# Moving narrowing calls between the first and the eighth expert, and the norm's squares to other buffers

## The chip, the cores and the metric

The kernel runs on one core of a Trainium2 chip. The metric is the device time of one execution in microseconds (us); lower is better. Engines are named as in the profile: PE multiplies matrices (PEld loads its weights), DVE, ACT and POOL work on vectors, SP issues transfers; ACT and POOL issue some too.

## The reference

Three layers follow one another. The second and third are what this change touches:

```python
# x: 3072 tokens x 384, from a gated linear attention in fp32
def _moe_ref(x, w_gate, w1, w2):          # 8 experts, 384 tokens each, chosen greedily by x @ w_gate
    ...
    for e in range(E):
        mask = assigned == e
        h = np.maximum(x[mask] @ w1[e], 0.0)      # 384 -> 1024
        out[mask] = h @ w2[e]                     # 1024 -> 384
    ...
def _moe2_ref(x, w_gate, w_val, w_out, rms_g):
    rms = np.sqrt(np.mean(x * x, axis=-1, keepdims=True) + 1e-06)
    xn = x / rms * rms_g
    g = xn @ w_gate                               # 384 -> 1536
    silu = g * (1.0 / (1.0 + np.exp(-g)))
    return (silu * (xn @ w_val) @ w_out).astype(np.float32)
```

The three weights of the last layer arrive as 64-bit floats and are made into 32-bit floats on the chip.

## The kernel before

**Products.** Each fp32 operand is split into a high part and the remainder; a product is three matmuls (`mm3`). The split of a weight piece of 128x1536 (768 KB), `piece_split`, is a cast on ACT (L880) and a subtraction (L883) on DVE, for two pieces of the last layer on POOL.

**Experts.** `expert(e)` runs eight slots j = 0 to 7, each on 128 of the 1024 hidden columns. PE computes h[j] (9 matmuls), ACT makes hh (L1161), DVE makes the remainder hl (L1162), and two slots later PE uses both in `second(e, j-2)` (9 matmuls). After h[j] is handled, `side(e, j)` adds the work for what comes next: gathering and turning the next expert's rows (`xpose`), loading and splitting weight pieces, and the narrowing. Each engine runs its instructions in the order in which this code is written.

**Narrowing.** The last layer's weights fall into 36 items, and one call of `narrow_step` does three things, each for another item:

```python
if len(done) > 1 or (done and not ready):
    nc.scalar.dma_start(*done.pop(0))          # write a finished item to DRAM (192 KB), issued by ACT
if len(ready) > 1 or (ready and not todo):
    done.append(narrow2(*ready.pop(0)))        # make a 32-bit item from a loaded one
if todo:
    ready.append(narrow(*todo.pop(0)))         # load a raw item (384 KB), issued by SP into nraw
```

`narrow2` is one multiplication on ACT into the buffer nr (L1080), three DVE instructions into nb and ne (L1081, L1082, L1084) and two POOL instructions on nr (L1085, L1086). An item is loaded in call n, made in call n+2 and written in call n+4; forty calls finish all. nraw and nr have three buffers each and nb two, given out in turn, so the multiplication of an item waits until the item that last used its nr buffer has landed in DRAM (ACT nr L1080 <- DMA w_o<-nr in the views).

**Eighth expert.** There `side` loads and splits the first pieces of the last layer (`w2_load`, `piece_split(W2[j-1])`), and prepares the norm of the first 256 tokens: `squares` in slot 0 (ACT: L983, two L986, and the cast L990; DVE: two additions L987 and a remainder L991), `total` in slot 2 (two PE matmuls L995, L996, and a square root with its table load, L997), then reciprocals, scaling, and in slot 6 a cast on ACT (L1019) and a remainder on POOL (L1020) for each of three parts. The squares are held in nraw buffers. After the eighth expert PE begins the last layer.

Of the kernel before, what the change touches and what calls it, by code (L numbers as in the profile page):

```python
# [7 lines left out]
F32 = mybir.dt.float32  # L8
F32R = mybir.dt.float32r
BF = mybir.dt.bfloat16  # L10
I32 = mybir.dt.int32
# [793 lines left out]
def tile_kernel(ctx, tc, q, k, v, f_logit, w_gate, w1, w2, w2_gate, w2_val, w2_out, rms_g, fT, kT, qT, vL, out):  # L805
# [70 lines left out]
    def piece_split(p, cp=None):  # L876
        pool, raw, shape, eng = p
        hi, lo = (pool.tile([128, 1536], F32R, name="w").rearrange("p (a b) -> p a b", a=shape[0]) for _ in range(2))
        if cp is None:
            nc.scalar.copy(hi, raw)  # L880
        else:
            cp.tensor_scalar(hi, raw, 1.0, 0.0, op0=OP.mult, op1=OP.add)
        eng.tensor_tensor(out=lo, in0=raw, in1=hi.bitcast(F32), op=OP.subtract)  # L883
        p[:] = [(hi, lo)]
# [17 lines left out]
    def gather(e):  # L902
        if e not in XG:
            XG[e] = [xp.tile([128, DM], F32, name="xrow") for _ in range(KD)]
        for c, t in enumerate(XG[e]):
            nc.gpsimd.indirect_dma_start(out=t, out_offset=None, in_=x_dram[:, :],
                                         in_offset=bass.IndirectOffsetOnAxis(
                                             ap=idx[:, 3 * e + c:3 * e + c + 1], axis=0))
# [3 lines left out]
    def w_load(e, i):  # L912
        W1[e, i] = piece(wpool, rawp, *w_src(e, i), nc.vector, e == 1 and i < 2)
# [10 lines left out]
    with ExitStack() as st:  # L924
        with tc.tile_pool(name="rw", bufs=8) as rw, tc.tile_pool(name="rwp", bufs=4, space=PSUM) as rwp:
# [8 lines left out]
            def side(s):  # L934
                if 0 < s < 5:
                    pool, raw, shape, _ = W1[0, s - 1]
                    hi, lo = (pool.tile([128, 1536], F32R, name="w").rearrange("p (a b) -> p a b", a=shape[0])
                              for _ in range(2))
                    nc.scalar.copy(hi, raw)
                    parts[s - 1] = hi, lo, raw  # L940
# [29 lines left out]
    TC = 256  # L970
# [45 lines left out]
    def prep(c, d, X, eng):  # L1016
        s = xn[:, d, c * TC:(c + 1) * TC]
        hi, lo = (t[:, d, 0:TC] for t in X)
        nc.scalar.copy(hi, s)  # L1019
        eng.tensor_tensor(out=lo, in0=s, in1=hi.bitcast(F32), op=OP.subtract)  # L1020

    W2 = {}
    with ExitStack() as c1:
        P = lambda name, bufs, **kw: c1.enter_context(tc.tile_pool(name=name, bufs=bufs, **kw))
        hp = P("m1h", 3, side="right")
        tp = P("m1t", 1, side="right")
        psT = P("m1psT", 2, space=PSUM)
# [4 lines left out]
        def w2_load(i):  # L1032
            if i < 7:
                W2[i] = piece(wpool, rawp, *w2_src(i), nc.gpsimd if i in (1, 3) else nc.vector)
# [3 lines left out]
        def xpose(e, d):  # L1038
            if d == 0:
                XT[e] = xt_tiles()  # L1040
            o = psT.tile([128, CAP], F32, name="xT")
            for c in range(3):
                nc.tensor.transpose(o[:, c * 128:(c + 1) * 128], XG[e][c][:, d * 128:(d + 1) * 128], ident)
            split(e, d, o)
# [15 lines left out]
        def nraw():  # L1060
            return tp.tile([128, 384, 2], I32, name="nraw", bufs=3)
# [30 lines left out]
        def narrow_step():  # L1092
            if len(done) > 1 or (done and not ready):
                nc.scalar.dma_start(*done.pop(0))
            if len(ready) > 1 or (ready and not todo):
                done.append(narrow2(*ready.pop(0)))
            if todo:
                ready.append(narrow(*todo.pop(0)))
# [4 lines left out]
            X0.extend(xt_tiles())  # L1103
            return [t[:, 0, 0:TC] for t in X0]

        n0 = Norm(0, tp, psT, "xT", lambda n: nraw().rearrange("p c two -> p (c two)").bitcast(F32)[:, :TC], first_parts)
        tail0 = n0.steps()[2:]
        NORM0 = {(E - 1, 0): [n0.squares], (E - 1, 2): [n0.total], (E - 1, 3): tail0[0:2], (E - 1, 4): tail0[2:3]}
        del tail0[:3]
# [1 line left out]
        def side(e, j):  # L1111
            if e + 1 < E:
                if j == 0:
                    gather(e + 1)
                    w_load(e + 1, 1)
                if j in ((1, 2, 3, 4, 5) if e == 0 else (1, 3, 5)):
                    narrow_step()
                if 0 < j < 5:
                    piece_split(W1[e + 1, j - 1])
                if j in (1, 2):  # L1120
                    w_load(e + 1, j + 1)
                if j > 4:
                    xpose(e + 1, j - 5)
                if j == 7:
                    if e + 2 < E:
                        w_load(e + 2, 0)
                    else:
                        w2_load(0)
                if j > 5:
                    narrow_step()  # L1130
            else:
                if j < 6:
                    w2_load(j + 1)
                if j in (0, 1, 3):
                    narrow_step()
                if j:
                    piece_split(W2[j - 1])
                if j == 5:
                    for f in tail0:
                        f()  # L1140
                if j == 6:
                    for d in range(KD):
                        prep(0, d, X0, nc.gpsimd)
            for f in NORM0.get((e, j), ()):
                f()
# [190 lines left out]
```

## Time and profile before

| what | value |
|---|---|
| median of three runs | 809.45 us (806.89 to 809.86) |
| the profiled execution | 806.72 us, of which its instructions span 805.0 us |
| PE busy | 784.6 us, 97% of the span |
| DVE, ACT, POOL busy | 474.7, 391.0 and 277.4 us |
| granted TensorE clock | 0.993 on average |

A busy share is an average over stages. Times in the rows further below are counted from the start of the span. The first expert runs from about 141 to 165 us, the eighth from about 324 to 351 us, and the last layer fills the rest.

### The profile page before, as it was taken

The numbers are of one execution on the slowest core, as the hardware profiler recorded it, in microseconds if no ns is written. First come the engines' busy times: TensorE is split into PE (matmuls) and PEld (weight loads), VectorE is DVE, ScalarE is ACT, GpSimd is POOL, SyncE is SP. The second block draws the span as 40 slices with busy tenths as digits, with TensorE's granted clock in tenths as the row PEclk, the third lists the DMA queues.
The fourth block names the chain that finished last, engine by engine and source line by source line (L and its number), as shares of the span: only waits on it lengthen the run. The fifth ranks groups of instructions, "written<-read, shape, count | busy, mean of one in ns | idle before, by whom it ended". The sixth has DMA issues, their size and how long they took to land.

```text
span 805.0 us, 17025 instructions
## 1 busy us (share of the span) xinstructions
PE 784.6 (97%) x6813; PEld 767.3 (95%) x6813; DVE 474.7 (59%) x855; ACT 391.0 (49%) x853; POOL 277.4 (34%) x332
## 2 busy tenths in 40 slices
PE   8999987999999999999999999999999999999996
PEld 7888876999999999999999999999999999999996
DVE  8999885988886768665434343444443443434331
ACT  5888571565456455764434343434434243434221
POOL 7889603377577667430111111110201011111110
PEclk9999997999999999999999999999999999999999
DMA  9999453697667866521000000000000000000000
GB/s 280 219 243 244 167 202 130 240 315 269 238 232 273 296 234 236 208 77 40 20 1 22 1 20 1 21 2 20 20 2 21 2 20 1 21 1 21 1 21 20
DMA packets 44278, 88.60 MB, mean 110 GB/s; under 512 B 5888, under 2 KB 23552, under 8 KB 44192
## 3 DMA queue, kind: packets, MB, share of 16 engines
q1 hardware_dynamic: 35088, 70.90, 27.8%
q0 software_dynamic: 3104, 9.44, 3.2%
q10 hardware_dynamic: 6000, 7.09, 2.5%
q8 instruction: 55, 0.90, 0.5%
q14 instruction: 31, 0.25, 0.1%
HBM read 70.91 MB, written 16.52 MB: 109 GB/s over the span
## 4 chain that ended last, share of the span: by engine, by line
PE 71%; issue 7%; DVE 2%; DMA 2%; POOL 1%; ACT 1%; POOLq 0%; DVEq 0%; ACTq 0%
PE o L686 5%; PE g L685 5%; PE g L686 5%; PE v L686 5%; PE v L687 5%; PE v L685 5%; PE g L687 5%; PE o L685 5%; PE o L687 5%; PE h L686 4%; PE h L687 4%; PE h L685 4%; PE x L686 3%; PE x L687 3%; PE x L685 3%
## 5 line engine op out<-in xcount | busy, mean ns | idle before, releaser
L1261 DVE TENSOR_TENSOR hf<-sg,v 128x256 f32<-128x256 f32 x144 | 59.9, 416 | 179.6 <-PE v L687 132.1
L1264 ACT CAST hh<-hf 128x256 fp32r<-128x256 f32 x144 | 58.6, 407 | 139.3 <-DVE hf L1261 139.3
L1020 POOL TENSOR_TENSOR xlo<-xn,xhi 128x256 fp32r<-128x256 f32 x36 | 29.6, 823 | 275.1 <-ACT xhi L1019 275.1
L686 PE MATMUL g<-xlo,w 128*128 128x256 f32 x432 | 119.3, 276 | 0.0
L685 PE MATMUL v<-xhi,w 128*128 128x256 f32 x432 | 119.2, 276 | 0.0
L686 PE MATMUL v<-xlo,w 128*128 128x256 f32 x432 | 119.2, 276 | 0.0
L687 PE MATMUL g<-xhi,w 128*128 128x256 f32 x432 | 119.2, 276 | 0.0
L687 PE MATMUL v<-xhi,w 128*128 128x256 f32 x432 | 119.2, 276 | 0.0
L685 PE MATMUL g<-xhi,w 128*128 128x256 f32 x432 | 119.2, 276 | 0.0
L1259 ACT ACTIVATE sg<-g 128x256 f32<-128x256 f32 x144 | 55.3, 384 | 98.8 <-PE g L687 98.5
L1265 DVE TENSOR_TENSOR hl<-hf,hh 128x256 fp32r<-128x256 f32 x144 | 61.3, 425 | 68.0 <-ACT hh L1264 63.3
L686 PE MATMUL o<-w,hh 128*128 128x384 f32 x288 | 97.0, 337 | 0.0
L685 PE MATMUL o<-w,hh 128*128 128x384 f32 x288 | 96.6, 335 | 0.0
L687 PE MATMUL o<-w,hl 128*128 128x384 f32 x288 | 96.2, 334 | 0.0
L685 PEld LDWEIGHTS g<-xhi,w 128*128 128x128 f32 x432 | 81.1, 188 | 0.0
L687 PEld LDWEIGHTS g<-xhi,w 128*128 128x128 f32 x432 | 81.1, 188 | 0.0
L685 PEld LDWEIGHTS v<-xhi,w 128*128 128x128 f32 x432 | 81.1, 188 | 0.0
L686 PEld LDWEIGHTS v<-xlo,w 128*128 128x128 f32 x432 | 81.1, 188 | 0.0
L687 PEld LDWEIGHTS v<-xhi,w 128*128 128x128 f32 x432 | 81.1, 188 | 0.0
L686 PEld LDWEIGHTS g<-xlo,w 128*128 128x128 f32 x432 | 81.0, 187 | 0.1
L883 DVE TENSOR_TENSOR w<-wraw,w 128x1536 fp32r<-128x1536 f32 x35 | 68.4, 1954 | 5.3 <-ACT w L880 4.9
L1085 POOL TENSOR_TENSOR nr<-nr,ne 128x384 f32<-128x384 f32 x36 | 52.1, 1446 | 56.3 <-DVE ne L1084 16.2
(247 smaller groups left out, 1869.0 us busy)
## 6 DMA issues: line engine op xcount, KB each, us to landing
wraw<-in_moe_w_dram SPq DMA_DIRECT2D x32, 768.0 KB
v<-in_v_rows_dram SPq DMA_DIRECT2D x16, 288.0 KB
x_dram<-xrows SPq DMA_DIRECT2D x24, 192.0 KB
nraw<-in_moe_w_gate_dram SPq DMA_DIRECT2D x12, 384.0 KB
nraw<-in_moe_w_val_dram SPq DMA_DIRECT2D x12, 384.0 KB
nraw<-in_moe_w_out_dram SPq DMA_DIRECT2D x12, 384.0 KB
raw_f<-in_f_logit_turned_dram SPq DMA_DIRECT2D x26, 144.0 KB
raw_k<-in_k_turned_dram SPq DMA_DIRECT2D x26, 144.0 KB
```

Source lines behind the costliest of these rows:

```text
L685: nc.tensor.matmul(out, lhs[0], rhs[0], start=first, stop=False)
L686: nc.tensor.matmul(out, lhs[0], rhs[1], start=False, stop=False)
L687: nc.tensor.matmul(out, lhs[1], rhs[0], start=False, stop=last)
L883: eng.tensor_tensor(out=lo, in0=raw, in1=hi.bitcast(F32), op=OP.subtract)
L1020: eng.tensor_tensor(out=lo, in0=s, in1=hi.bitcast(F32), op=OP.subtract)
L1085: nc.gpsimd.tensor_tensor(out=r, in0=r, in1=e2.bitcast(F32), op=OP.mult)
L1259: nc.scalar.activation(sg, pg, AF.Silu)
L1261: nc.vector.tensor_tensor(out=h, in0=sg, in1=pv, op=OP.mult)
L1264: nc.scalar.copy(hh, h)
L1265: nc.vector.tensor_tensor(out=hl, in0=h, in1=hh.bitcast(F32), op=OP.subtract)
```

## The change

The number of calls stays forty. Slot 5 of expert 0 (in the code e == 0, j == 5) loses its call. In expert 7 the calls were in slots 0, 1 and 3; they are now in slots 1, 2, 4 and 6. Every call after slot 4 of expert 0 therefore handles the item that the call before it had handled. The squares take buffers from nr (the sum) and nb (the two further squares) and none from nraw.

```diff
@@ -1103,7 +1103,12 @@
             X0.extend(xt_tiles())
             return [t[:, 0, 0:TC] for t in X0]
 
-        n0 = Norm(0, tp, psT, "xT", lambda n: nraw().rearrange("p c two -> p (c two)").bitcast(F32)[:, :TC], first_parts)
+        def first_tmp(n):
+            t = tp.tile([128, 384], F32, name="nr", bufs=3) if n == "ss" else \
+                tp.tile([128, 384], I32, name="nb", bufs=2).bitcast(F32)
+            return t[:, 0:TC]
+
+        n0 = Norm(0, tp, psT, "xT", first_tmp, first_parts)
         tail0 = n0.steps()[2:]
@@ -1113,7 +1118,7 @@
-                if j in ((1, 2, 3, 4, 5) if e == 0 else (1, 3, 5)):
+                if j in ((1, 2, 3, 4) if e == 0 else (1, 3, 5)):
                     narrow_step()
@@ -1131,7 +1136,7 @@
             else:
                 if j < 6:
                     w2_load(j + 1)
-                if j in (0, 1, 3):
+                if j in (1, 2, 4, 6):
                     narrow_step()
```

On DVE in expert 0, before, from hl of slot 5 to hl of slot 7 (hl is L1162, the narrowing L1081 to L1084, the turned rows' remainder L1049):

```order
L1162 SCALAR_TENSOR_TENSOR hl_3343<-h_3332,hh_3342 128x384
L1081 TENSOR_SCALAR nb_3356<-nraw_3288 128x384
L1082 SCALAR_TENSOR_TENSOR nb_3356<-nraw_3288,nb_3356 128x384
L1084 TENSOR_SCALAR ne_3357<-nb_3356 128x384
L1049 TENSOR_TENSOR xlo_3368<-xT_3369,xhi_3367 128x384
L1162 SCALAR_TENSOR_TENSOR hl_3386<-h_3375,hh_3385 128x384
L1049 TENSOR_TENSOR xlo_3368<-xT_3398,xhi_3367 128x384
L1081 TENSOR_SCALAR nb_3405<-nraw_3326 128x384
L1082 SCALAR_TENSOR_TENSOR nb_3405<-nraw_3326,nb_3405 128x384
L1084 TENSOR_SCALAR ne_3406<-nb_3405 128x384
L1162 SCALAR_TENSOR_TENSOR hl_3427<-h_3416,hh_3426 128x384
```

And the same place now (lines below the first edit carry numbers higher by five):

```order
L1167 SCALAR_TENSOR_TENSOR hl_3343<-h_3332,hh_3342 128x384
L1049 TENSOR_TENSOR xlo_3356<-xT_3357,xhi_3355 128x384
L1167 SCALAR_TENSOR_TENSOR hl_3374<-h_3363,hh_3373 128x384
L1049 TENSOR_TENSOR xlo_3356<-xT_3386,xhi_3355 128x384
L1081 TENSOR_SCALAR nb_3393<-nraw_3288 128x384
L1082 SCALAR_TENSOR_TENSOR nb_3393<-nraw_3288,nb_3393 128x384
L1084 TENSOR_SCALAR ne_3394<-nb_3393 128x384
L1167 SCALAR_TENSOR_TENSOR hl_3415<-h_3404,hh_3414 128x384
```

Of the two sets of three narrowing instructions between hl of slot 5 and hl of slot 7, the one behind slot 5 is gone.

On ACT in expert 7, before, from the end of slot 0 (its write and its multiplication L1080, then the squares) through hh of slots 1 and 2 to the second weight split:

```order
L1094 DMA w32_o_64<-nr_5207 128x384
L1080 ACTIVATE nr_5300<-nraw_5214 128x384
L983 ACTIVATE nraw_5307<-xn_3105 128x256
L986 ACTIVATE nraw_5309<-xn_3105 128x256
L986 ACTIVATE nraw_5312<-xn_3105 128x256
L990 CAST xhi_5315<-nraw_5307 128x256
L1161 ACTIVATE hh_5329<-h_5319 128x384
L1094 DMA w32_o_64<-nr_5250 128x384
L880 CAST w_5336<-wraw_5245 128x1536
L1161 ACTIVATE hh_5350<-h_5340 128x384
L880 CAST w_5365<-wraw_5295 128x1536
```

And now, at the same place:

```order
L983 ACTIVATE nr_5287<-xn_3105 128x256
L986 ACTIVATE nb_5289<-xn_3105 128x256
L986 ACTIVATE nb_5292<-xn_3105 128x256
L990 CAST xhi_5295<-nr_5287 128x256
L1166 ACTIVATE hh_5309<-h_5299 128x384
L1094 DMA w32_o_64<-nr_5195 128x384
L1080 ACTIVATE nr_5318<-nraw_5202 128x384
L880 CAST w_5325<-wraw_5233 128x1536
L1166 ACTIVATE hh_5339<-h_5329 128x384
L1094 DMA w32_o_64<-nr_5238 128x384
L1080 ACTIVATE nr_5357<-nraw_5245 128x384
L880 CAST w_5364<-wraw_5285 128x1536
```

The multiplication ahead of the squares is gone, and one now stands ahead of each of the two weight splits. With three nr buffers given out in turn (..., nr_5195, nr_5238, nr_5287 for the squares, nr_5318, nr_5357), nr_5318 is the memory of nr_5195 and nr_5357 that of nr_5238, which the write just ahead of each multiplication reads.

## Rows read from the trace of the kernel before

**Rows 1.** Waits of PE, whole run: us in total, times, longest.

```profile
PE xT L995 <- ACT xhi L990: 1.3, 1, 1.3
PE x L686 <- DVE hl L1162: 1.1, 1, 1.1
```

**Rows 2.** Timeline of DVE, expert 0: start, duration, what, idle before.

```profile
157.66 0.55 DVE L1162 SCALAR_TENSOR_TENSOR hl<-h,hh 128x384 fp32r<-128x384 f32 x1
158.12 0.71 DVE L1081 TENSOR_SCALAR nb<-nraw 128x384 int32<-128x384 int32 x1
158.87 1.25 DVE L1082 SCALAR_TENSOR_TENSOR nb<-nraw,nb 128x384 int32<-128x384 int32 x1
160.22 0.36 DVE L1084 TENSOR_SCALAR ne<-nb 128x384 int32<-128x384 int32 x1
...
164.04 0.55 DVE L1162 SCALAR_TENSOR_TENSOR hl<-h,hh 128x384 fp32r<-128x384 f32 x1
```

**Rows 3.** Timeline of PE, turn of expert 7's slots 2 and 3, and its last hl.

```profile
329.59 0.34 PE L686 MATMUL x<-hl,w 128*128 128x384 f32 x1
329.77 0.34 PE L687 MATMUL x<-hh,w 128*128 128x384 f32 x1
331.43 0.39 PE L995 MATMUL xT<-xhi,onesr 128*128 128x256 f32 x1 [1.32 <-ACT xhi L990]
...
332.11 0.34 PE L685 MATMUL h<-xhi,w 128*128 128x384 f32 x1
...
349.45 0.34 PE L686 MATMUL x<-hl,w 128*128 128x384 f32 x1
```

**Rows 4.** Timeline of ACT, expert 6's slot 7 to expert 7's slot 3.

```profile
320.61 0.33 ACTq L1094 DMA_DIRECT2D w_o<-nr  x1
...
327.57 0.55 ACT L1080 ACTIVATE nr<-nraw 128x384 f32<-128x384 uint32 x1 [1.14 <-DMA w_o<-nr]
328.02 0.40 ACT L983 ACTIVATE nraw<-xn 128x256 f32<-128x256 f32 x1
...
330.97 0.40 ACT L990 CAST xhi<-nraw 128x256 fp32r<-128x256 f32 x1 [1.93 <-DVE nraw L987]
330.98 0.33 ACTq L1094 DMA_DIRECT2D w_o<-nr  x1
...
331.66 1.47 ACT L880 CAST w<-wraw 128x1536 fp32r<-128x1536 f32 x1
...
333.41 1.48 ACT L880 CAST w<-wraw 128x1536 fp32r<-128x1536 f32 x1
...
336.94 1.48 ACT L880 CAST w<-wraw 128x1536 fp32r<-128x1536 f32 x1
```

**Rows 5.** Timeline of DVE, expert 7.

```profile
328.76 2.17 DVE L987 TENSOR_TENSOR nraw<-nraw 128x256 f32<-128x256 f32 x2 [0.40 <-ACT nraw L986]
...
338.44 1.76 DVE L883 TENSOR_TENSOR w<-wraw,w 128x1536 fp32r<-128x1536 f32 x1 [0.80 <-ACT w L880]
...
342.68 2.71 DVE L883 TENSOR_TENSOR w<-wraw,w 128x1536 fp32r<-128x1536 f32 x1
...
348.72 0.55 DVE L1162 SCALAR_TENSOR_TENSOR hl<-h,hh 128x384 fp32r<-128x384 f32 x1
```

**Rows 6.** The tile ss: the same additions of squares in the last layer (min/median/max ns).

```profile
L987 DVE TENSOR_TENSOR ss<-ss,hf x22: 424/426/428, 355.5 to 726.1; 128x256 f32<-128x256 f32 x22
```

**Rows 7.** Windows in expert 7: busy time per engine, PEclk, DMA share, GB/s.

```profile
332.00:332.25 0.25, 0.25 (x2) 0.25 (x3) 0.25 (x1) 0.25 (x1) 0.00 (x0) 1.00 1.00 362
332.25:332.50 0.25, 0.25 (x4) 0.25 (x3) 0.10 (x1) 0.25 (x1) 0.00 (x0) 1.00 0.61 205
332.50:332.75 0.25, 0.25 (x3) 0.25 (x2) 0.00 (x0) 0.25 (x1) 0.00 (x0) 1.00 0.00 0
```

**Rows 8.** Timeline of SP's queue, expert 6's slots 6 and 7.

```profile
315.89 1.33 SPq L873 DMA_DIRECT2D wraw<-w_g  x3
```

**Rows 9.** Timeline of POOL, expert 7.

```profile
334.96 3.51 POOL L883 TENSOR_TENSOR w<-wraw,w 128x1536 fp32r<-128x1536 f32 x1 [4.31 <-ACT w L880]
```

## The prediction

> **What bounds the kernel now.** I read the page first: PE is at work for nearly the whole span. So I went to the list of waits, for PE. Of its sixteen entries, two lie in the experts and none in the last layer [rows 1]: 1.1 us for hl and 1.3 us for the operand of the norm's total. The timelines place them. The first is in expert 0: hl of slot 7 starts on DVE at 164.04 and ends at 164.59, when PE has been waiting for it [rows 2]. DVE ran without a pause from hl of slot 5 to there, and the narrowing of slot 5 took it from 158.12 to 160.58. So in this slot DVE is the bound. The second is in expert 7 [rows 3]: the matmul of `second` at 329.77 is followed by the total at 331.43 and by h[3] at 332.11. Matmuls follow each other here every 0.18 us (329.59 to 329.77), so without a wait the total's two and h[3] would have begun by 330.3, three steps after 329.77: this place costs PE 1.8 to 1.9 us, and I carry 1.9.
>
> Why the total is late is read from ACT [rows 4]. The multiplication at 327.57 waited for a write issued at 320.61, and the squares, begun at 328.02, come behind it. From the squares' start to the cast at 330.97 there are 2.95 us, and 2.17 of them are two DVE additions [rows 5].
>
> What comes next in expert 7 matters as much. ACT then works without a pause from 330.97 to the third weight split at 336.94, and DVE, which waits for that split at 338.44, has no pause from there to hl of slot 7 at 348.72 [rows 5]. That hl ends at 349.27 and PE uses it at 349.45 [rows 3]: PE and the chain ACT, DVE end expert 7 within 0.2 us of each other. Whatever PE gains at the total is worth nothing unless this chain comes earlier too, and whatever delays the third split ends on PE.
>
> **The change part by part.** *Slot 5 of expert 0.* Ahead of hl of slot 7, DVE loses three instructions. They took 2.46 us by their place on the timeline; the same three, by the shortest of their durations there for the last and half or less for the first two, would be 1.3 us, when POOL does not work beside them. Either is enough for the 1.1 us of wait. I count −1.1 us. The bounds are 0, if something else arrives last, and −1.3, with the matmul's own step of 0.18 us on top. Between expert 0 and expert 7 the calls do the same work on other items, and PE waits nowhere there [rows 1], so I cost that at nothing; without this cover a late hl would be paid at the 1.1 us of expert 0.
>
> *Squares.* Their multiplication and POOL's two additions of narrowing no longer lie in slot 0. The DVE additions, 1.04 us each today beside POOL, took 0.43 us each in the last layer, where no narrowing runs [rows 6]. So the way from the squares to the cast shrinks by 1.3 us. When do the squares begin? Their sum now takes the nr buffer that the write of expert 6's slot 7 reads, so they wait for a landing, as the multiplication did. The write issued at that place today landed at 327.5, 6.9 us after its issue [rows 4]: it stood behind the three big loads issued from 315.89 [rows 8] and a fourth. Now a raw load of 384 KB is queued by SP in front of all but the first of these; at the 362 GB/s of [rows 7] it is worth 1.1 us. So the squares begin between 327.5 and 328.6, and I take 328.0, as today.
>
> *Two multiplications behind writes.* In slots 1 and 2 of expert 7 the multiplication waits for the write that ACT issued just before. Let L be the time from issue to landing. Behind the waiting instruction stand the weight split, hh of the next slot, the table load and root, and hh of slot 3. The row for L is the write issued at 330.98 [rows 4] into empty queues: its bytes move until 332.5 [rows 7]. So L is above 1.5 us. The upper bound is the 6.9 us of a write behind big loads. At 330 the big loads are over, so I take a value near the lower one, 2.0 us. It is an estimate: 1.5 us plus some time for the landing to be signalled.
>
> The Trainium skill, in DMA: Bandwidth & Descriptors, section Anatomy of one DMA, gives about 2.0 us of fixed cost plus the bytes at 436 GB/s, most of the fixed part being the receipt of the write; that fit is for transfers that POOL issues. For 192 KB it makes an estimate of L = 2.45 us, where the row shows only the 1.5 us until the last byte; with it the sum below would come out 0.7 us higher.
>
> The first write leaves when the cast at 330.97 starts, since ACT issues a transfer while earlier instructions still run (the write at 330.98). The split that began at 331.66, 0.69 us after the cast, now begins after L and a multiplication of 0.45 us (327.57 to 328.02): L − 0.24, or 1.76 us later. The second write leaves when the first has landed; until its landing ACT has a multiplication (0.45) and a split with an hh (1.75, from 331.66 to 333.41) to do, 2.2 us, so for L below 2.2 only the second multiplication counts, 0.45 us. Together ACT is 2.2 us later. For L = 1.5 it is 1.7.
>
> *POOL beside DVE.* The additions of two items now run on POOL in slots 1 to 3, ahead of the weight remainder that begins at 334.96 [rows 9] and takes 3.51 us. The second of them can't begin before its multiplication and DVE's three instructions (1.3 us or more), and each addition takes about 1 us, as the DVE additions beside them did [rows 5]: from a second multiplication that ends near 335 that makes about 338 to 339 for the remainder, an estimate. So it moves beside the DVE split that begins at 338.44. That split took 1.76 us with POOL idle; the one at 342.68, beside POOL, took 2.71 [rows 5]. I add 0.95 us, bounds 0 and 2.85 for three such splits.
>
> The third split in expert 7, and with it the DVE chain, comes 0 (start of the squares) − 1.3 + 2.2 = 0.9 us later, plus 0.95 for the contention, less the 0.18 us between hl and its use: PE ends expert 7 1.7 us later than today. The 1.9 us at the total are mostly freed, but PE then waits for hl of slots 2 to 7 instead. Writes in slots 4 and 6 wait for items finished long before. They end before the load that reads them in the last layer, so I cost them at nothing; uncovered, the load would be late by one L, 2.0 us.
>
> **Sum.** −1.1 + 1.7 = +0.6 us. On the profiled execution's 806.72 us it gives 807.3; the median of the runs shown is 2.7 us above that execution, and against it the forecast is 810.0 us. A change within 0.5%, 4 us here, is about what a measurement of this kernel cannot tell from none.
>
> **Rivals.** *Both stalls vanish (chance 0.26).* If POOL does not disturb DVE and the squares start early (the write of slot 7 put ahead of the last big load, at about 326 us), the chain comes 2 us earlier and covers the two waits: −1.1 − 1.9 = −3.0, 806.4 us. For it: the raw load splits the big loads, so the write may be issued before the last of them. Against it: SP needs about 0.45 us for each issue [rows 8], which puts the last of them just before the write.
>
> *POOL against DVE (0.09).* With three splits lengthened instead of one the sum is 2 × 0.95 higher: +2.5 us, 812.0. The Trainium skill's GPSIMD Engine Reference, section Key points, says that POOL shares its SBUF interfaces with DVE instructions that read two SBUF inputs, as these splits do; the 1.76 and 2.71 us of [rows 5] agree. By that rule every split beside a POOL instruction pays, and it would give this rival's time. Against it: POOL's two remainders lie beside DVE work today as well.
>
> *Writes behind loads (0.05).* This one ends slower. If big loads are still in the queues at 330 us, L is 6.9 us. The first wait then costs 6.66, the second 0.45 + 6.9 − 2.2 = 5.15, the chain 0.9 − 2.2 + 11.8 = 10.5 us, and the total is −1.1 + 10.5 + 0.95 − 0.18 = +10.2: 819.7 us. It decides from about L = 3.8 us on, where 2L − 2.0 for the two waits brings the sum to +4 us. Against it: the queues are empty at 332.5 [rows 7] and the next big load needs a buffer that the delayed split frees.
>
> *Nothing gained in expert 0 (0.05).* If another instruction, say a turned row's remainder, is last there, the −1.1 is missing: 811.1 us.
>
> **How the numbers follow.** The forecast has 0.55, the rivals 0.26, 0.09, 0.05 and 0.05. All but the writes behind loads stay within 4 us. The forecast's own range is the spread of its terms, L from 1.5 to 2.45 and the squares' start by 0.5 us either way, about 808 to 812. To hold 8 in 10 I reach to the first rival's 806.4 below and past the second's 812.0 above, by the 0.8 us that a late POOL costs: 806.2 to 812.8. Faster by over 0.5% needs more than both stalls: 0.05, for what the terms leave out. Slower by over 0.5%: 0.05 for the late writes and 0.03 for three terms at their upper bounds together. Same: 0.87.
>
> **What would show it.** In expert 0 PE's wait for hl of slot 7 is gone and the experts 0 to 6 end about 1.1 us earlier. The two additions of squares take 0.43 us each, and PE's wait at the total falls below 0.9 us. ACT shows two new waits for w_o<-nr in slots 1 and 2 of expert 7, of 1 to 2 us each, the third split comes later relative to the squares' cast than today's 5.97 us, by about 2.2, and PE waits for hl two or three times in slots 2 to 7. The prediction is wrong if the third split follows the cast by less than 7 us (L is smaller, and the first rival holds) or by more than 10 us, or if the stretch from 165 us to the eighth expert changes its length.

## The result, and the profile after

The changed kernel took 813.17 us (median of 6 runs, 812.86 to 813.77), the kernel before 808.63 us beside it (6 runs, 806.31 to 809.86): ratio 1.0053, 95% interval 1.0035 to 1.0071. It is 4.5 us slower; 0.6 us were forecast, and the range ended at 812.8.

The profiled execution spans 812.1 us, 7.1 more than before's. Cut at PE's first h of expert 0, its last `second` matmul of experts 0 and 6, and its first g of the last layer, the spans show where (PE makes the first two h of expert 0 in smaller pieces, so this cut lies ahead of the 141 us given for the first expert above):

| stage | before, us | after, us |
|---|---|---|
| up to expert 0 | 136.60 | 138.34 |
| expert 0 | 29.36 | 28.04 |
| experts 1 to 6 | 157.44 | 158.52 |
| expert 7 | 27.42 | 32.88 |
| last layer | 454.18 | 454.29 |

The first stage holds the same code in all kernels here, and lay anywhere between 136.6 and 139.3 us in the eighteen profiles. Experts 1 to 6 took 156.8 to 159.0 us in all but two. So these two rows tell nothing; expert 0 (−1.3) and expert 7 (+5.5) do, and add up to 4.1.

The waits of PE, answering to [rows 1]:

```profile
PE x L686 <- DVE hl L1167: 3.8, 2, 3.3
...
PE xT L995 <- ACT xhi L990: 0.3, 1, 0.3
```

Expert 0's wait for hl is gone, the wait at the total fell from 1.3 to 0.3 us, and one new wait of 3.3 us for hl stands in expert 7. ACT's timeline there, answering to [rows 4]:

```profile
322.10 0.33 ACTq L1094 DMA_DIRECT2D w_o<-nr  x1
...
329.66 0.42 ACT L983 ACTIVATE nr<-xn 128x256 f32<-128x256 f32 x1 [2.31 <-DMA w_o<-nr]
...
331.40 0.40 ACT L990 CAST xhi<-nr 128x256 fp32r<-128x256 f32 x1 [0.71 <-DVE nr L987]
331.50 0.33 ACTq L1094 DMA_DIRECT2D w_o<-nr  x1
331.71 0.48 ACT L1166 ACTIVATE hh<-h 128x384 fp32r<-128x384 f32 x1
333.39 0.55 ACT L1080 ACTIVATE nr<-nraw 128x384 f32<-128x384 uint32 x1 [1.19 <-DMA w_o<-nr]
...
339.68 1.48 ACT L880 CAST w<-wraw 128x1536 fp32r<-128x1536 f32 x1
```

The squares wait 2.31 us for a write issued 7.5 us earlier. The first multiplication waits 1.19 us for a write issued at 331.50, 1.87 us before. The third split begins at 339.68. DVE and POOL from there on, answering to [rows 5] and [rows 9]:

```profile
341.19 1.93 DVE L883 TENSOR_TENSOR w<-wraw,w 128x1536 fp32r<-128x1536 f32 x1 [0.81 <-ACT w L880]
...
345.60 2.50 DVE L883 TENSOR_TENSOR w<-wraw,w 128x1536 fp32r<-128x1536 f32 x1
348.03 4.47 DVE L1005 SCALAR_TENSOR_TENSOR xn<-xn,gcol,nr 128x256 f32<-128x256 f32 x3
352.42 0.54 DVE L1167 SCALAR_TENSOR_TENSOR hl<-h,hh 128x384 fp32r<-128x384 f32 x1
352.89 2.19 DVE L883 TENSOR_TENSOR w<-wraw,w 128x1536 fp32r<-128x1536 f32 x1
355.00 0.55 DVE L1167 SCALAR_TENSOR_TENSOR hl<-h,hh 128x384 fp32r<-128x384 f32 x1
...
335.35 2.62 POOL L1086 TENSOR_TENSOR nr<-nr,nb 128x384 f32<-128x384 f32 x1
...
341.45 9.97 POOL L883 TENSOR_TENSOR w<-wraw,w 128x1536 fp32r<-128x1536 f32 x2
```

POOL's two remainders now run back to back from 341.45 to 351.42, and the three scalings, 1.27 us together before, take 4.47. First their row in the kernel before, then the view of their line now:

```profile
345.31 1.27 DVE L1005 SCALAR_TENSOR_TENSOR xn<-xn,gcol,nraw 128x256 f32<-128x256 f32 x3
```
```profile
L1005 DVE SCALAR_TENSOR_TENSOR xn<-xn,gcol,nr x3: 471/472/3678, 348.0 to 352.0; 128x256 f32<-128x256 f32 x3
```

(shortest, median and longest in ns). Two took 0.47 us, one 3.68: it ended 0.3 us after POOL's second remainder, and hl of slot 6, behind the three, came at 352.42. PE waits for that hl and then has half its clock for some 3 us (timeline of PE, then windows: busy time of PE, PEld, DVE, ACT, POOL, the granted clock, DMA share, GB/s):

```profile
349.33 0.34 PE L685 MATMUL x<-hh,w 128*128 128x384 f32 x1
353.02 0.45 PE L686 MATMUL x<-hl,w 128*128 128x384 f32 x1 [3.34 <-DVE hl L1167]
...
354.25 0.53 PE L685 MATMUL x<-hh,w 128*128 128x384 f32 x1
354.57 0.53 PE L686 MATMUL x<-hl,w 128*128 128x384 f32 x1
...
357.78 0.28 PE L685 MATMUL g<-xhi,w 128*128 128x256 f32 x1
```
```profile
350.00:352.00 2.00, 0.00 (x0) 0.00 (x0) 2.00 (x2) 1.12 (x1) 1.42 (x1) 1.00 1.03 392
352.00:354.00 2.00, 0.98 (x5) 0.98 (x6) 2.00 (x4) 2.00 (x6) 1.27 (x2) 0.92 0.33 51
354.00:356.00 2.00, 2.00 (x7) 1.63 (x6) 2.00 (x3) 1.02 (x1) 2.00 (x2) 0.50 0.83 283
356.00:358.00 2.00, 2.00 (x10) 2.00 (x10) 1.29 (x1) 0.99 (x3) 1.88 (x1) 0.73 0.23 85
```

A second path ends at nearly the same place. The sixth weight piece is loaded into the buffer that POOL's first remainder reads. SP issued this load at 346.52, just after that remainder ended at 346.48, and ACT waited 5.82 us for its landing (waits of SP in total, times, longest; then ACT's timeline):

```profile
SPq L873 <- POOL w L883: 9.0, 1, 9.0
```
```profile
350.88 1.47 ACT L880 CAST w<-wraw 128x1536 fp32r<-128x1536 f32 x1 [5.82 <-DMA wraw<-w_v]
```

In the kernel before, this load left at 338.50, and the cast, at 343.62, did not wait for it. Now DVE's split of the piece began at 352.89 and could not have begun before the cast ended at 352.35. So if only the hold at the scaling were gone, the end of DVE's chain would come only about 0.5 us earlier, an estimate from these rows. POOL's late remainders delay expert 7 in both ways.

Expert 7 can thus be cut in three by one rule for every kernel: **A** from expert 6's last `second` matmul to the third weight split on ACT, **B** from there to hl of slot 7 on DVE, **C** from there to PE's first g. Before: 13.53 + 11.78 + 2.11 = 27.42 us. After: 14.78 + 15.32 + 2.78 = 32.88. Of the 5.46 us, ACT's lateness is 1.25, DVE's longer chain 3.54, PE's end 0.67.

### The profile page after: what moved, and what is told of

Read it like the earlier page. It is cut to its first block, busy times and chain, and to the rows that moved or that the text cites. A ratio compares the mean times of both kernels' runs of the same rounds, so it can differ in the third digit from the quotient of the medians.

```text
span 812.1 us, 17027 instructions
## 1 busy us (share of the span) xinstructions
PE 789.2 (97%) x6813; PEld 770.9 (95%) x6813; DVE 472.8 (58%) x855; ACT 391.9 (48%) x853; POOL 281.8 (35%) x332
## 4 chain that ended last, share of the span: by engine, by line
PE 82%; issue 7%; DMA 4%; DVE 4%; ACT 1%; POOL 1%; POOLq 0%; SPq 0%; DVEq 0%; ACTq 0%
PE o L686 5%; PE g L685 5%; PE g L686 5%; PE v L687 5%; PE g L687 5%; PE v L685 5%; PE v L686 5%; PE o L685 5%; PE o L687 5%; PE x L686 4%; PE h L686 4%; PE x L687 4%; PE x L685 4%; PE h L687 4%; PE h L685 4%
## 5 line engine op out<-in xcount | busy, mean ns | idle before, releaser
L1020 POOL TENSOR_TENSOR xlo<-xn,xhi 128x256 fp32r<-128x256 f32 x36 | 29.5, 821 | 274.5 <-ACT xhi L1019 274.5
L1085 POOL TENSOR_TENSOR nr<-nr,ne 128x384 f32<-128x384 f32 x36 | 53.8, 1495 | 64.0 <-ACT hh L1166 31.7
```

What stands on the lines that cost most here:

```text
L1085: nc.gpsimd.tensor_tensor(out=r, in0=r, in1=e2.bitcast(F32), op=OP.mult)
```

## The experiments

Two theories stood at the start: ACT's waits for landings make the end of expert 7 late (A in the expectations), or POOL's weight remainders do, which come late and stand beside DVE's last work (P). Each ratio is against runs of the kernel before on the same chip; A, B, C and the length of expert 7 are from the profile.

| kernel | us | ratio (95%) | A | B | C | expert 7 |
|---|---|---|---|---|---|---|
| e0_alone | 808.34 | 0.9993 (0.9979 to 1.0006) | 12.63 | 11.78 | 2.37 | 26.78 |
| e7_alone | 813.87 | 1.0063 (1.0044 to 1.0082) | 15.03 | 14.86 | 3.10 | 32.99 |
| squares_alone | 810.78 | 1.0026 (1.0011 to 1.0041) | 13.92 | 11.79 | 2.19 | 27.90 |
| sum_in_nraw | 808.29 | 0.9996 (0.9982 to 1.0011) | 11.85 | 15.61 | 2.13 | 29.59 |
| items_in_nraw | 812.12 | 1.0042 (1.0025 to 1.0060) | 13.01 | 16.08 | 2.79 | 31.88 |
| three_pieces | 812.87 | 1.0053 (1.0034 to 1.0072) | 15.40 | 15.44 | 2.40 | 33.24 |
| split_first | 812.16 | 1.0036 (1.0021 to 1.0051) | 13.80 | 16.63 | 2.10 | 32.53 |
| raw_and_split_first | 809.29 | 1.0009 (0.9995 to 1.0023) | 11.03 | 16.58 | 2.10 | 29.71 |
| raw_and_three_pieces | 809.23 | 1.0020 (1.0002 to 1.0039) | 12.31 | 14.88 | 3.09 | 30.28 |
| no_pool_additions | 805.59 | 0.9964 (0.9948 to 0.9980) | 11.17 | 12.80 | 2.11 | 26.08 |
| no_dve_narrowing | 805.02 | 0.9962 (0.9947 to 0.9977) | 11.57 | 12.19 | 2.10 | 25.86 |
| changed_no_additions | 809.69 | 1.0008 (0.9987 to 1.0028) | 15.36 | 12.77 | 2.10 | 30.23 |
| changed_dve_remainders | 809.09 | 1.0002 (0.9983 to 1.0021) | 14.07 | 12.94 | 2.10 | 29.11 |
| raw_and_dve_remainders | 806.96 | 0.9984 (0.9969 to 0.9998) | 11.40 | 13.31 | 2.10 | 26.81 |
| none_in_eighth | 807.05 | 0.9984 (0.9973 to 0.9995) | 10.15 | 12.26 | 3.08 | 25.49 |
| none_in_eighth_dve | 807.27 | 0.9986 (0.9972 to 1.0001) | 10.15 | 12.48 | 2.86 | 25.49 |

Single profiles differ by themselves: e0_alone has the code of the kernel before in expert 7 and took 0.65 us less there (A 12.63 instead of 13.53), and e7_alone has that of the changed kernel and differs by up to 0.5 us in A and B. A difference of less than about 1 us between two profiles therefore shows little.

**The parts alone.** e0_alone is the kernel before without the call in expert 0's slot 5, which goes to expert 1's slot 4; e7_alone is the changed kernel with that call put back and one taken from expert 1; squares_alone is the kernel before with the squares in nr and nb.

```diff
# e0_alone, against before
-                if j in ((1, 2, 3, 4, 5) if e == 0 else (1, 3, 5)):
+                if j in ((1, 2, 3, 4) if e == 0 else (1, 3, 4, 5) if e == 1 else (1, 3, 5)):
# e7_alone, against the changed kernel
-                if j in ((1, 2, 3, 4) if e == 0 else (1, 3, 5)):
+                if j in ((1, 2, 3, 4, 5) if e == 0 else (1, 3) if e == 1 else (1, 3, 5)):
```

> The change in expert 0 alone: slot 5 has no narrowing call, expert 1 gets a call more (slot 4), and expert 7 and the squares' buffers are as before. Theory P (the time was lost in expert 7 alone, where POOL's long remainders meet DVE): expert 0 ends 1.1 to 1.3 us earlier, expert 7 keeps its length of 27.4 us, and the run is 0 to 1.3 us faster than before, since PE's slower pace between experts 1 and 6 may give back up to 1.1 us. Rival A (the time was lost because ACT is late in expert 7): the same here. Rival Q (the shift of all later calls by one costs time between expert 1 and 6): the run stays as much faster as expert 0 is, 1.3 us, because the calls from expert 2 on are where they were.

> The change in expert 7 and the squares' buffers alone: expert 0 keeps seven calls, expert 1 has one fewer (none in slot 5), expert 7 has slots 1, 2, 4 and 6. Theories P and A: expert 7 is 4.5 to 5.5 us longer than before, PE's wait of 1.1 us in expert 0 is there again, and the run is 5 to 6 us slower than before. Rival Q: less than half of that.

> The squares' buffers alone: the kernel before with the sum of squares in an nr buffer and the two further squares in nb buffers; all forty calls in their old slots. The last square then waits for POOL's second addition of the item made just before it (330.65 us in the trace of before), so the cast behind the squares comes about 0.5 to 1 us later than before, and the total too. Theory P: POOL's two weight remainders begin as before, within 1 us, and the run is 0.5 to 1.5 us slower. Rival A: every us that ACT is later arrives at the end of expert 7 too, so the same size; the two differ here only in what POOL does.

Expert 0 took 28.00 us in e0_alone and 29.11 in e7_alone: the 1.1 us between them, 1.36 against the kernel before, are gained by the missing call. The run time of e0_alone does not show them clear of noise (0.9993, 0.9979 to 1.0006). e7_alone has the whole loss (32.99 us in expert 7). In squares_alone one of the squares waits for POOL, which still reads the nb buffer it takes:

```profile
333.87 0.42 ACT L986 ACTIVATE nb<-xn 128x256 f32<-128x256 f32 x1 [2.00 <-POOL nr L1086]
```

This run is about 2.1 us slower (0.9 to 3.3), a little more than expected; its expert 7 is 0.5 us longer in the profile. So the buffers alone make the smaller part of the loss, and the larger lies in where expert 7's calls stand, together with the buffers.

**The waits for landings.** sum_in_nraw keeps the sum of the squares in nraw, items_in_nraw makes the last two items in nraw instead of nr. The first frees the squares (and, since nr is then turned over one buffer later, most of both multiplications) from the landings, the second only the multiplications.

```diff
# sum_in_nraw
-            t = tp.tile([128, 384], F32, name="nr", bufs=3) if n == "ss" else \
+            t = nraw().rearrange("p c two -> p (c two)").bitcast(F32) if n == "ss" else \
# items_in_nraw
-            r = tp.tile([128, n], F32, name="nr", bufs=3)
+            r = tp.tile([128, n], F32, name="nr", bufs=3) if todo else \
+                nraw().rearrange("p c two -> p (c two)").bitcast(F32)[:, :n]
```

> The changed kernel with one buffer different: the sum of squares takes an nraw buffer, so no square and neither multiplication in slots 1 and 2 of expert 7 waits for a write that was issued just before. Rival A (ACT's waits for landings carry the loss): those waits, 2.3 and 1.2 us, go, the third weight split comes 3 to 4 us earlier than in the changed kernel, and the run is 4 to 7 us faster than it, level with before or better. Theory P (POOL's remainders stand behind the additions of two items, begin late, and hold up DVE when both read the buffers): the split of ACT comes as much earlier, but POOL's remainders still begin after 337 us, one of them still lies over the scaling L1005, and at least 2 us of the loss against before stay.

> The changed kernel with the last two items made in nraw buffers that nobody reads any more, so that their multiplications wait for no write, while the squares' sum still waits for the write out of its nr buffer. In the changed kernel the squares waited 2.31 us, the first multiplication 1.19, the second not at all. If each wait counts as ACT loses it, the third weight split comes 1.2 us earlier than 339.68 with the squares still near 329.7, PE's longest wait for hl falls to about 2.1 us, too short for the clock to fall as in sum_in_nraw and split_first, and expert 7 takes 30 to 31.7 us instead of 32.9. Rival: the squares' wait alone sets the end, and expert 7 stays within 0.5 us of 32.9, with the low clock after the wait.

In sum_in_nraw the squares begin 2.33 us after expert 6's end, instead of 4.76, A shrinks by 2.9 us, and the ratio falls from 1.0053 to 0.9996. But B is as long as in the changed kernel: POOL's remainders and the scaling look the same, and the split of the sixth piece even waited for its late cast.

```profile
344.58 4.49 DVE L1005 SCALAR_TENSOR_TENSOR xn<-xn,gcol,nraw 128x256 f32<-128x256 f32 x3
...
349.89 1.76 DVE L883 TENSOR_TENSOR w<-wraw,w 128x1536 fp32r<-128x1536 f32 x1 [0.34 <-ACT w L880]
...
338.01 9.99 POOL L883 TENSOR_TENSOR w<-wraw,w 128x1536 fp32r<-128x1536 f32 x2
```

In items_in_nraw the third split follows the cast by 6.88 us instead of 8.28, as expected, but expert 7 gains only 1.0: POOL's additions (two now 2.4 and 2.5 us long, beside DVE) come late, its remainders run beside the scaling again (4.46 us), and PE waits once for 3.8 us, then at half the clock. The expectation of a short wait missed: B grew by 0.8 us. So the waits for landings are a cause, and not the only one.

**POOL's long remainders: their order and size.** three_pieces makes each remainder of 128x1536 on POOL three instructions of 128x512; split_first puts the weight split ahead of the narrowing in expert 7. Both were also run with the sum in nraw.

```diff
# three_pieces, in piece_split
-        eng.tensor_tensor(out=lo, in0=raw, in1=hi.bitcast(F32), op=OP.subtract)
+        n = 3 if eng is nc.gpsimd else 1
+        for i in range(n):
+            s = slice(i * 1536 // n, (i + 1) * 1536 // n)
+            f = lambda t: t.rearrange("p a b -> p (a b)")[:, s]
+            eng.tensor_tensor(out=f(lo), in0=f(raw), in1=f(hi).bitcast(F32), op=OP.subtract)
# split_first, in side
-                if j in (1, 2, 4, 6):
-                    narrow_step()
                 if j:
                     piece_split(W2[j - 1])
+                if j in (1, 2, 4, 6):
+                    narrow_step()
```

> The changed kernel, with each of POOL's two weight remainders in expert 7 issued as three instructions over a third of the columns. Theory P (a POOL instruction that is running keeps DVE's two-input instructions out until it ends): the scaling L1005, whose first instruction took 3.7 us beside a POOL remainder of 5.0 us, now waits for a third of one, so the three take at most 3 us; PE's wait for hl, 3.3 us, falls below 1.5, and the run is 1.5 to 3 us faster than the changed kernel. If the two engines only shared bandwidth, or under rival A (ACT's waits for landings carry the whole loss), the three scalings and PE's wait stay as they are, within 0.5 us.

> The changed kernel with two statements exchanged in expert 7: the weight split stands ahead of the narrowing call, so POOL's remainder stands ahead of the two additions of the item made in that slot. Theory P (POOL's remainders come late because they stand behind additions): the first remainder begins before 338 instead of at 341.5 us, the sixth piece lands in time and ACT's wait of 5.8 us for it falls below 2, and the run is 2 to 4 us faster than the changed kernel. Rival A: ACT has the same two waits for landings ahead of the third split, so the run stays within 1 us of the changed kernel.

> Both edits: the sum of squares in an nraw buffer, and the weight split ahead of the narrowing call in expert 7. If the loss is the sum of two parts, the waits for landings and POOL's late remainders, expert 7 is no longer than before (27.4 us) and the run is 1 to 3 us faster than before. If one part alone carried it, this run is no faster than the better of the two single edits.

> The sum of squares in an nraw buffer, and POOL's weight remainders in three instructions each. Theory P: what was left of the loss with the nraw buffer alone, PE's waits of 2.6, 0.5 and 0.5 us in and behind expert 7, falls to below 1.5 us in all, and the run is 1 to 2.5 us faster than with the nraw buffer alone. Rival A, and shared bandwidth: no difference to that run, within 1 us.

Pieces changed nothing in the sum: six of them took 10.87 us and the scaling 4.31, PE's wait stayed at 3.4. That is what the expectation gave for shared bandwidth, but the three scalings are not slowed alike in the changed kernel (3.68, 0.47, 0.47 us), and with pieces each of them waits for one piece:

```profile
L1009 DVE SCALAR_TENSOR_TENSOR xn<-xn,gcol,nr x3: 1478/1483/1504, 348.2 to 351.0; 128x256 f32<-128x256 f32 x3
```

In split_first the scaling is back at 1.3 us, but B is 16.63. The first remainder began at 339.96, where before 338 was expected, and it now holds up another DVE instruction, whose usual 0.36 us become 3.44. The sixth piece was in time here (its cast waited for no transfer), so the holds on DVE alone can make B that long.

```profile
340.52 3.44 DVE L1084 TENSOR_SCALAR ne<-nb 128x384 int32<-128x384 int32 x1
...
339.96 3.79 POOL L883 TENSOR_TENSOR w<-wraw,w 128x1536 fp32r<-128x1536 f32 x1
...
348.14 1.47 ACT L880 CAST w<-wraw 128x1536 fp32r<-128x1536 f32 x1
```

My theory that the scaling beside POOL was the loss fell in this form: moving the collision moves PE's wait (here 2.7, 0.4, 1.1 and 0.4 us for hl, 3.8 in the changed kernel) and does not shorten it. On top of the nraw buffer neither edit won anything: expert 7 took 29.71 and 30.28 us, against 29.59 with the buffer alone.

**Taking work away.** no_pool_additions and no_dve_narrowing start from sum_in_nraw, changed_no_additions from the changed kernel. All three leave out a part of the arithmetic of the last two items.

```diff
# no_pool_additions, changed_no_additions
-            nc.gpsimd.tensor_tensor(out=r, in0=r, in1=e2.bitcast(F32), op=OP.mult)
-            nc.gpsimd.tensor_tensor(out=r, in0=r, in1=b.bitcast(F32), op=OP.add)
+            if todo:
+                nc.gpsimd.tensor_tensor(out=r, in0=r, in1=e2.bitcast(F32), op=OP.mult)
+                nc.gpsimd.tensor_tensor(out=r, in0=r, in1=b.bitcast(F32), op=OP.add)
# no_dve_narrowing: with todo empty, in place of the three DVE and two POOL instructions
+                nc.gpsimd.tensor_tensor(out=r, in0=r, in1=r, op=OP.mult)
+                nc.gpsimd.tensor_tensor(out=r, in0=r, in1=r, op=OP.add)
```

> The sum of squares in nraw as in sum_in_nraw, and POOL's two additions (L1085, L1086) of the last two items left out, so these two items are written without their upper half; DVE's and ACT's part of them stays. sum_in_nraw's expert 7 took 29.6 us, before's 27.4. Theory P (the rest of the loss, 2.2 us, is POOL's: its additions push its weight remainder beside DVE's scaling): the remainder begins near 336 instead of 338.0, the scaling's three take under 3.5 us instead of 4.49, expert 7 takes 27.4 to 28.2 us, and the ratio to before is 0.997 to 0.998. Theory D (the rest is DVE's own narrowing work, six instructions of 2.9 us in sum_in_nraw's timeline, put in front of a chain without pauses): expert 7 stays at 29.0 to 29.6 us, ratio 0.999 to 1.000.

> The sum of squares in nraw as in sum_in_nraw, and DVE's three instructions of the last two items left out (POOL multiplies and adds the item with itself instead, two instructions of the same shape), so these two items hold other numbers. Theory D: DVE's chain in expert 7 comes up to 2.9 us earlier, PE's waits for hl shrink, expert 7 takes 27.0 to 28.0 us, ratio to before 0.996 to 0.998. Theory P: POOL's additions still come late, expert 7 stays at 28.8 us or more, ratio 0.999 to 1.000.

> The changed kernel with POOL's two additions (L1085, L1086) of the last two items left out, so these two items are written without their upper half; all waits for landings stay. If landings and additions each carry a share of their own (32.9 to 29.6 by the landings, 29.6 to 26.1 by the additions), expert 7 takes about 29.4 us. If POOL's remainders, pushed late beside DVE's scaling, are the larger cause: the first begins near 337.5 instead of 341.45, the scaling's three take under 1.5 us instead of 4.47, PE's longest wait for hl is under 1.5 us, the clock does not fall, and expert 7 takes 28.7 us or less (before's chain of 27.4 plus the 1.25 us by which the third split is later than before, counted from the end of expert 6). If the landing waits alone are the cause: 31 us or more.

Either half gone, expert 7 falls by 3.5 and 3.7 us, more than either expectation, so the first two did not tell P from D (D: DVE's own narrowing work). They show why: what counts is when POOL's remainder falls. In no_pool_additions it still stops DVE, just as long, but in a slot where the hl behind it was not yet needed, and PE does not wait:

```profile
332.59 3.89 DVE L1082 SCALAR_TENSOR_TENSOR nb<-nraw,nb 128x384 int32<-128x384 int32 x1
...
332.55 3.51 POOL L883 TENSOR_TENSOR w<-wraw,w 128x1536 fp32r<-128x1536 f32 x1 [6.65 <-ACT w L880]
```

In changed_no_additions the same pair (3.75 and 3.50 us) stands at 338.4 and costs PE 1.5 us, since ACT is late there: 30.23 us. That is above the 29.4 of two shares that add up and below the 31 of landings alone. In these runs the sixth piece also comes in time: ACT's longest wait for it is 0.3 us.

**The remainders on DVE.** The same work, and no long POOL instruction in expert 7 until L1020:

```diff
-                W2[i] = piece(wpool, rawp, *w2_src(i), nc.gpsimd if i in (1, 3) else nc.vector)
+                W2[i] = piece(wpool, rawp, *w2_src(i), nc.vector)
```

> The changed kernel with the remainders of the last layer's pieces 1 and 3 on DVE instead of POOL: the same work and the same waits for landings, 3.5 us more of it on DVE (two more splits of 1.76), and no long POOL instruction beside DVE. If a remainder on POOL holds DVE up for nearly as long as it runs (scaling 4.47 instead of 1.27, splits 1.93 and 2.50 instead of 1.76), DVE loses about as much as it gains: scaling 1.27, splits 1.76 each, expert 7 between 31.5 and 33.5 us. If DVE and POOL only slow each other a little, DVE's chain is longer by the 3.5 us: expert 7 takes 35 us or more.

> The changed kernel with the sum of squares in nraw (as sum_in_nraw) and the remainders of pieces 1 and 3 on DVE (as changed_dve_remainders). If the two causes add up, expert 7 takes 29.6 + 29.1 - 32.9 = 25.8 us, and the ratio to before is 0.996 to 0.998. If they share the 1.9 us of the low clock, which either of them takes away, it is 27.7 us, ratio 0.998 to 0.9995. If one of them does what the other does, 29 us.

With two more remainders of about 1.75 us on DVE, B is 2.4 us shorter and expert 7 3.8 us shorter, better than both expectations. The waits for landings were left as they were (1.6 and 1.2 us), and PE's longest wait is 1.0. The edit takes away both ways in which POOL was late: no remainder holds DVE, and the load of the sixth piece leaves at 338.50, so that ACT waits 0.1 us for it. No run takes away the one and leaves the other at the end of expert 7.

```profile
346.77 1.26 DVE L1005 SCALAR_TENSOR_TENSOR xn<-xn,gcol,nr 128x256 f32<-128x256 f32 x3
```
```profile
PE x L686 <- DVE hl L1167: 2.0, 4, 1.0
```

Without landings' waits and without long remainders expert 7 takes 26.81 us. One cure gives 3.3, the other 3.8, both 6.1: they share 1.0 us, between the two expectations and no more than two profiles of the same code can differ by. The 1.9 us that the expectation gives to the low clock is shown by no run: with the low clock gone C fell by 0.7.

**No item in the eighth.** Calls in slots 1 to 4, 6 and 7 of experts 0 to 2, and in expert 7 two that only write; then the same with the remainders on DVE.

```diff
-                if j in ((1, 2, 3, 4, 5) if e == 0 else (1, 3, 5)):
+                if j in ((1, 2, 3, 4) if e < 3 else (1, 3, 5)):
...
-                if j in (0, 1, 3):
+                if j in (0, 1):
```

> The kernel before, with calls in slots 1 to 4, 6 and 7 of experts 0, 1 and 2, as before in experts 3 to 6, and in slots 0 and 1 of expert 7: forty calls, and those in expert 7 only write, no item is made there. The squares are in nraw. If the loss in expert 7 is the narrowing that stands in it, then without any of it the squares start without the 1.14 us wait and the 0.45 us multiplication, the additions take 0.43 us each, PE's wait at the total is gone, DVE's chain comes 2 to 3 us earlier; expert 7 takes 25.5 to 26.8 us instead of 27.4, expert 0 28.0 instead of 29.4, the ratio to before is 0.995 to 0.998. Rival: DVE's other work in expert 7 sets its end, it stays at 27.0 us or more, and only expert 0's 1.3 us remain: ratio 0.998 to 1.000, as e0_alone (0.9993).

> The kernel none_in_eighth with the remainders of pieces 1 and 3 on DVE. There POOL's first remainder lies where DVE waits for ACT, and the second beside a split of 2.06 us; expert 7 took 25.5 us with 1.1 us of PE's waits for hl. If a remainder on POOL costs only where DVE has work beside it, DVE on its own takes 3.5 us more here and gets back less than 1 us: expert 7 stays at 25.3 us or comes to 27 us, ratio to before 0.997 to 1.000. If POOL's long instructions cost wherever they stand, it falls below 25.3 us, ratio under 0.998.

Expert 7 takes 25.49 us with the remainders on either engine. On POOL the first runs here where DVE waits for ACT, and the second mostly beside reciprocals and hl, which are not held; on DVE they fit into the time in which DVE waited. The run gains less than experts 0 and 7 do (1.4 and 1.9 us), since the added calls cost experts 1 and 2 about 1.6 us: 26.80 and 27.61 us, where the others took 26.42. none_in_eighth and raw_and_dve_remainders, both at 0.9984 with intervals that end below 1, are faster than the kernel before by 0.16% and faster than the changed one.

## Why the prediction was wrong

**Slot 5 of expert 0**, −1.1: right, −1.32 in the profile, and by that edit (−1.36 in e0_alone).

**Squares**: right. The additions took 0.95 us for two, the cast followed the squares' start by 1.74 us instead of 2.95 (−1.2, forecast −1.3). The start, taken as unchanged, was 4.76 us after expert 6's end instead of 4.61. One of the first rival's two conditions was even met: SP issued its last load at 322.44, after the write at 322.10. The write landed no earlier for it, 7.5 us after its issue, and the gain of that rival did not come. What stood at the squares anyway was a landing: before it held the multiplication in front of them.

**Two multiplications behind writes**, +2.2 with L = 2.0: right. L was 1.87 us, nearer to the 2.0 carried than to the upper end of 2.45, and the third split followed the cast by 8.28 instead of 5.97 us, +2.31. Together A grew by 1.25 us, where 0.9 was forecast.

**POOL beside DVE**, +0.95 with bounds 0 and 2.85: this step failed. B grew by 3.54 us. It is the sum over four rows: the splits at 341.19 (+0.17), 345.60 (−0.21) and 352.89 (+0.37), and the scaling (+3.20). The price was read wrongly from [rows 5]. The split of 2.71 us at 342.68 was no split made slower by 0.95; it was held until POOL's second remainder, not shown then, was done:

```profile
340.25 3.52 POOL L883 TENSOR_TENSOR w<-wraw,w 128x1536 fp32r<-128x1536 f32 x1 [1.78 <-ACT w L880]
```

This one ended at 343.77, and the split 1.62 us later. The 0.95 was about what was left of POOL's instruction when the split came (1.09 us), so its bound is the 3.5 us of POOL's instruction, not a number per split: DVE rows of 3.44, 3.68, 3.75 and 3.89 us stand beside POOL rows of 3.5 to 5 us. POOL is held in turn: the addition at 335.35 took 2.62 us beside a split. The remainders began 16.55 us after expert 6's end (341.45), and not 14.6 to 15.6 after it (338 to 339 in the times of the kernel before). The second multiplication ended as forecast, 11.35 instead of 11.6 us after expert 6, but the three DVE instructions of its item stood behind that split and an hl for 1.24 us more. And [rows 9] lay at 334.96 to 338.47 in the kernel before, where DVE, but for two hl, waited for ACT until 338.44 [rows 5]: its cover was an idle DVE, and the delay took it away. The prediction named the queue and the order and did not ask what DVE does in the 3.5 us when POOL's instruction comes. Nor did it ask which load waits for the buffer that a late remainder frees: the sixth piece's load left 6.5 us later than before, counted from expert 6's end, and this second path ends within about 0.5 us of the first. The runs bear out that POOL's late remainders are the cause of B's growth: the work left as it was and the remainders off POOL, B falls by 2.4 us although DVE has 3.5 us more to do in expert 7. How much of it is the hold and how much the late piece stays open.

The rival *POOL against DVE* (812.0, chance 0.09) had the mechanism and the nearest time; it counted three splits at 0.95, not the scaling at the full length. The Trainium skill's SBUF — State Buffer, section Who interferes with whom, says that a DVE instruction with two SBUF inputs and a GpSimd (POOL) instruction that reads SBUF block each other whole, whichever comes first holding the ports to its end. The traces agree, in both directions (3.68 us for a scaling of 0.47, 2.62 for an addition of 1.02). An estimate by that rule, with the 3.51 us of [rows 9], is up to 3.5 us for one meeting instead of 0.95, and the sum would have been +0.6 + 2.6 = +3.2 us.

**The end**, "less the 0.18 us between hl and its use": C grew by 0.67 us, for PE's clock was at half after the 3.34 us wait. No term was there for it. It costs little, because hl of slot 7 came only at 355.00.

The sum in expert 7 was +1.7 and is +5.46: the missing 3.8 are 0.35 from A, 2.6 from B and 0.85 from the end (0.67, and the 0.18 counted as a gain). Since the waits at landings and POOL's blocks meet in one chain, either cure alone takes away more than half; neither alone is "the" cause. Of the signs that the prediction named for being wrong, the first two did not come (the third split followed the cast by 8.28 us, between 7 and 10), and the third, a changed length of experts 1 to 6, came by 1.1 us, which profiles of the same code differ by too; none of them looked at POOL. That the first stage and experts 1 to 6 differ by some us between profiles of the same code was not traced further.

## What to carry to other kernels

Where POOL works beside DVE instructions of the kind held here (two inputs in SBUF, and the integer narrowing), price a meeting as the time that the other's instruction still has to run, and look on the timeline at what DVE does in exactly that stretch; a long POOL instruction that is free in an idle slot of DVE can cost nearly its whole length when it is pushed out of it (3.2 of 3.5 us here). Ask as well which load waits for the buffer that the late instruction reads. Work that is "off the path" is best moved to a place where no chain of two engines ends at PE's next operand: with no item made in the last expert the same forty calls gave 0.9984 instead of 1.0053. A buffer taken from a ring that transfers read turns its next user into one that waits for a landing.

## What the hardware showed unexpectedly

A one-input integer instruction on DVE (L1084, 0.36 us alone) took 3.44 us beside POOL, while reciprocals (0.6 to 0.7 us, one operand, in SBUF) and hl (0.5 us, its h in PSUM) kept their times beside the same remainders. Cutting POOL's instruction in three let DVE in after each piece, but the next piece held the next DVE instruction, and the three scalings took 4.31 us instead of 4.47.

PE's clock fell to half, 1.2 GHz, after waits of 3.30 to 3.82 us in four kernels; after 2.72 us it fell in raw_and_three_pieces, and after 2.73 us it did not in split_first. In the changed kernel the step between two matmuls of 384 columns was then 0.32 us (354.25 to 354.57), where it is 0.18 in [rows 3].

The same write of 192 KB landed 1.87 us after its issue at 331.50, and 7.5 us after it at 322.10, among the big loads that SP issued from 317.96 to 322.44. And without any wait of PE, one expert took 26.14 us in some executions and 26.42 in others, with the same code (raw_and_dve_remainders 198.08 to 224.22, changed_no_additions 197.67 to 224.09, at the first `second` matmul of experts 2 and 3).
